# A recurrent-attention and mixture-of-experts kernel: another written-out order for its first ten steps

## The chip, the cores and the metric

The kernel runs on one core of a Trainium2 chip. The metric is the device time of one execution in microseconds (us), start to end. A core has four engines that each work through an instruction queue of their own, in order: PE (matrix products), DVE (vector work), ACT (pointwise functions, also used for copies) and POOL (general work; here also the issue of scattered writes). SP is a fifth queue that only issues transfers. An instruction starts when it is at the head of its queue and the semaphores it waits for have come.

## The reference

The first half is a gated recurrent attention over 4 batches, 8 heads, 768 tokens and 48 dimensions; the second routes each token to one of 8 experts.

```python
f = 1.0 / (1.0 + np.exp(-f_logit))
state = np.zeros((B, H, D, D))
for t in range(S):
    state = f[:, :, t, :, None] * state + np.einsum('bhd,bhe->bhde', k[:, :, t], v[:, :, t])
    y[:, :, t] = np.einsum('bhd,bhde->bhe', q[:, :, t], state)
x = y.transpose(0, 2, 1, 3).reshape(3072, 384)
logits = x @ w_gate                       # (3072, 8)
expert_idx = np.argmax(logits, axis=1)
gate_w = softmax(logits)[expert_idx]
out = gate_w * (np.maximum(x @ w1[expert_idx], 0) @ w2[expert_idx])   # per expert, 384 -> 1024 -> 384
```

## The kernel before

The tokens are cut into twelve units (u = 0 to 11), each 128 tokens of two batches with all heads. A unit has two halves, a and b, of four head pairs each. The recurrence inside a unit becomes matrix products; between units a state is carried, with two chains (units of equal parity follow each other). All steps below are written in program order under a manual schedule, so what stands first in the program stands first in each engine's queue.

The work of one unit, with the short names that the changed kernel gives it:

- SP: `lf`, `lk`, `lq`, `lv` load f, k, q, v (0.5, 0.5, 0.5 and 0.375 MB). Buffers are few (f 2, k 3, q 4, v 3), so a load waits until the unit that used the buffer has been read.
- ACT: `exp` and `ln` (log of the decay, L495 and L503), later `r` (growth, L524) and `dec` (decay, L539), both from the running sum; `keep` copies the turned k out of PSUM (L582), `set` copies y out of PSUM (L652), `lay` copies rows out (L707, L712).
- DVE: `sum` (running sum by a scan, L510), `q` (q times decay, L551), `mx` and `my` (causal masks of the two heads of a half, L568), `upd` (new state, L642 or L644), `lg` (logits, L690), and the routing chains `oh` (choose an expert, L228 to L236) and `place` (positions, L247 to L274).
- POOL: `kr` (k times growth, L528; for units 0 and 3 it runs on DVE instead, `krv`), the small copies `ends` (L534) and `last` (L546), the state's decay `upd..p` (L646), `line` (token numbers of a group), and `send`: two scattered row writes to `xs` in memory (L195).
- PE: `sc` (scores, L562), `kp` (k turned by the identity, L577), `wi` (y from inside the unit, L590), `dp` (the state's increment, L627), `bef` (y from the carried state, L611), `xp` (rows and logits from y, L682; every second unit two small counting products, L240 and L241).

Step n works on several units at once: PE does `sc(n)`, `kp(n)`, `wi(n-1)` first half, `xp(n-2)`, `wi(n-1)` second half, `dp(n)`, `bef(n-1)`. Steps 1 to 3 have extra conditions of their own in the loop (`if n == 1`, `1 < n < 4`, ...); from step 4 on all steps are alike until step 10. Two units make a group, whose tokens are routed together and sent by scatters in later steps.

PSUM sets two rings. `sc` takes four banks, two for each half, so a half's scores need the masks of the same half one unit earlier. `kp` a and b, `xp` a and b and `dp` take turns in two banks (`turns`), so each of them needs the last but one of that list to have been read: by `keep`, by `lg` and `lay`, or by `upd`. The output `yt` of `wi` and `bef` is one tile of two banks, a half in each.

Some `kr` are made to wait for a DVE instruction by hand, with the reason given as "the port of both":

```python
        def by_r(u, part=whole, on=nc.gpsimd):
            k = units[u]["k"][:, part]
            ins = on.tensor_tensor(k, k, units[u]["r"][:, part], op=OP.mult).ins
            if routed and on is nc.gpsimd:
                tc.add_manual_dep(ins, routed.pop().name, SYNC, reason="the port of both")
```

Before the first scores PE runs 24 products on zeros (`warm(24)`, L729, called `fill24` below), and 8 more after `kp(0)`.

After the twelve units come two steps without new units, with the first products of experts 0 and 1 (their rows are read back from `xs` as `xrow`, L289, which waits for the scatters sent so far), and then the eight experts in a row, all on PE (L336, L352, L1121, L1147). The first two experts' weights `w1t` and `w2t` are loaded at the end of steps 8 and 9.

Of the kernel before, what the change touches and what calls it, by code (L numbers as in the profile page):

```python
# [19 lines left out]
C = 128  # L20
# [100 lines left out]
def kernel(  # L121
# [318 lines left out]

    with ExitStack() as st:
# [7 lines left out]
        yt = psy.tile([128, 2, HP, C], F32, name="yt")  # L449
        nc.vector.memset(yt, 0.0)  # L450
# [119 lines left out]
        def keys(u):  # L570
            x = units[u]
            x["kn"] = wk.tile([128, SEG, C], F32, name="kn", bufs=1)
            x["kp"] = []
            for a in range(2):
                kp = turns("kp", [128, HP, C])
                for p in range(HP):
                    nc.tensor.transpose(kp[:, p], x["k"][:, HP * a + p], ident)  # L577
                x["kp"].append(kp)

        def keep(u):  # L580
            for a in range(2):
                nc.scalar.copy(units[u]["kn"][:, HP * a : HP * a + HP], units[u]["kp"][a])  # L582

        def within(u, a):

            x = units[u]
            if a == 0:
                x["yt"] = yt
            for p, h, _ in heads():
                nc.tensor.matmul(  # L590
                    x["yt"][DP * (h ^ a) : DP * (h ^ a) + D, a, p],
                    lhsT=x["v"][:, a, 2 * p + h],
                    rhs=x["at"][:, a, h, p],
                    start=p == 0,
                    stop=x["old"] is None,
                    skip_group_check=True,
                )

        def before(u):
# [6 lines left out]
            for p in range(HP):  # L606
                for h in range(2):
                    for a in range(2):
# [3 lines left out]
                            x["yt"][to : to + D, a, p],  # L612
# [7 lines left out]
        def added(u):  # L620
# [3 lines left out]
            for a in range(2):  # L624
                for p, h, r in heads():
# [3 lines left out]
                        lhsT=x["kn"][:, s, r],  # L629
# [6 lines left out]
        def update(u):  # L636
# [3 lines left out]
            last = _bc(x["last"], 2, D)  # L640
# [5 lines left out]
            return lambda: nc.gpsimd.tensor_tensor(new, new, last, op=OP.mult)  # L646

        def settle(u):
            x = units[u]
            x["ys"] = wk.tile([128, 2, HP, C], F32, name="ys", bufs=1)  # L650
            for a in range(2):
                nc.scalar.copy(x["ys"][:, a], x["yt"][:, a])  # L652
# [10 lines left out]
        def rows(u, counted=None):  # L663
# [11 lines left out]
            x["xr"], x["xp"] = group["xr"][:, 2 * (u - g[0]) :], []  # L675
            for a in range(2):
                j = 2 * (u - g[0]) + a
                xp, counts = pair()
                if a and counted:
                    counted.count(counts[:, :, 0 : counted.n])  # L680
                for p in range(HP):
                    done["rows"] = nc.tensor.matmul(  # L682
                        xp[:, p],
                        lhsT=x["ys"][:, a, p],
                        rhs=wx[:, p, 0:XW] if a else wx[:, p, E:WX],
                        start=True,
                        stop=True,
                    ).ins
                gate = slice(0, E) if a else slice(2 * D, XW)
                nc.vector.reduce_sum(  # L690
                    group["lg"][:, j],
                    xp[:, :, gate].rearrange("p h e -> p e h"),
                    axis=AX_X,
                )
                x["xp"].append(xp)
# [4 lines left out]
        def lay(u):  # L700

            x = units[u]
            for a in range(2):
                to = x["xr"][:, a, 0:DM].rearrange("p (h w) -> p h w", h=HP)
                if a:
                    for h in range(2):
                        nc.scalar.copy(  # L707
                            to[:, :, D * h : D * h + D],
                            x["xp"][a][:, :, XW - D * h - D : XW - D * h],
                        )  # L710
                else:
                    nc.scalar.copy(to, x["xp"][a][:, :, 0 : 2 * D])  # L712
# [4 lines left out]
        load(0, "f", ab)  # L717
        load(0, "k")
        load(1, "f", ab[:1])
        load(0, "q")  # L720
        load(1, "f", ab[1:])
        load_first_consts()
        load(1, "kq")
        for i in (1, 0):
            nc.gpsimd.memset(scores[i], 0.0)
        def warm(count):

            for _ in range(count):
                nc.tensor.matmul(yt[:, 0, 0], lhsT=pad[:, 0:C], rhs=pad[:, 0:C], start=True, stop=True)  # L729

        warm(24)
        for part in ab:
            steps(0, part)
            total(0, part)
        load(2, "f")
        load(0, "v")
        for part in ab:
            growth(0, part)
            by_r(0, part, nc.vector)
            decay(0, part)  # L740
        for part in ab:
            by_decay(0, part)
        ends(0)
        last_decay(0)
        lay_selection()
        for part in ab:
            steps(1, part)
        load(3, "f")
        load(2, "k")
        load(1, "v")  # L750
        load(2, "q")
        load_gate()
# [42 lines left out]
        score(0, 0)  # L795
        score(0, 1)
        keys(0)
        warm(8)
        for part in ab:
            total(1, part)  # L800
        for a, part in enumerate(ab):
            growth(1, part)
            by_r(1, part)
            decay(1, part)
            for h in range(2):
                mask(0, a, h)
            scaled = by_decay(1, part)
            if a == 0:
                routed.append(scaled)
        ends(1)  # L810
        last_decay(1)
        steps(2)
        load(4, "f")
        load(3, "k")
        load(3, "q")
        load(2, "v")
        total(2)
        keep(0)
        steps(3, logs=False)
        growth(2)  # L820
        load(5, "f")
        load_consts()

        for n in range(1, NU + 2):
            here, back, last = n, n - 1, n - 2
            ahead = n + 1 < NU
            state = n < NU - 2
# [3 lines left out]
            if 2 < last:  # L831
                settle(last)
# [5 lines left out]
            if ahead and not 1 < n < 4:  # L838
                by_r(n + 1)
                ends(n + 1)  # L840
# [9 lines left out]
            if n == 1:  # L850
                units[0]["old"] = None
                added(0)
                update(0)()
            if ahead and not 1 < n < 4:
                decay(n + 1)
                last_decay(n + 1)
            if state:
                keys(here)
                keep(here)
            if 1 < n < 4:  # L860
                growth(n + 1)
                if n == 3:
                    by_r(n + 1)
                ends(n + 1)
                decay(n + 1)
                last_decay(n + 1)
            if here < NU:
                for a in range(2):
                    for h in range(2):
                        if n == 2 and a and h:  # L870
                            by_r(n + 1, on=nc.vector)
                        mask(here, a, h)
            if n == 1:
                log(3)
                within(0, 0)
                within(0, 1)
                settle(0)
            if n == 1:
                steps(4, logs=False)
            elif n > 3 and n + 3 < NU:  # L880
                steps(n + 3)
# [3 lines left out]
            if 3 < n < NU - 2:  # L885
                total(n + 2)
            if n == NU - 2:
                by_decay(n + 1)
            first_half = 1 < n < NU - 2
            if first_half:  # L890
                within(back, 0)
            if 0 <= last:
                rt = rows(last, later[1] if later else None)
                lay(last)
            if 1 < n < 4:
                log(n + 2)
                steps(n + 3, logs=False)
# [5 lines left out]
            if ahead and n < NU - 2:  # L903
                by_decay(n + 1)
            if n == 2:
                total(n + 2)
            if rt and n != 3:
                rt.choose()
                if 3 < n < NU - 2:
                    routed.append(rt.latest)  # L910
                if n >= NU - 1:
                    rt.weigh()
            if later:
                settled(*later)
                routed.append(later[1].latest)
                later = None
            for a in range(int(first_half), 2):
                if 0 < back < NU:
                    within(back, a)
            if n == 2:  # L920
                settle(1)
            if n + 2 < NU and n > 3:
                growth(n + 2)
# [4 lines left out]
            if state:  # L928
                added(here)
                decayed = update(here)  # L930
            if n == 1:
                total(3)
            if n == 3:
                total(5)
                rt.choose()
                routed.append(rt.latest)
            if back < NU:
                before(back)
            if n == 3:
                settle(2)  # L940
                log(6)
                growth(5)
# [425 lines left out]
```

## Time and profile before

| | us |
|---|---|
| three runs of the kernel | 389.91, 390.06, 401.82 |
| their median | 390.06 |
| the profiled execution, its own time | 393.27 |
| its span, first to last instruction | 391.5 |
| PE busy in the span | 377.9 (97%) |
| DVE, ACT, POOL busy | 171.0, 102.8, 113.7 |
| scores of unit 0 start | 9.94 |
| scores of unit 2 start | 23.88 |
| scores of unit 10 start | 99.16 |
| first full expert product (L336, `hps`) | 144.59 |

The mean granted TensorE clock is 0.996. The attention part is the first third of the span; the rest is the experts. Times in the trace are counted from the span's start. A line of the timeline gives start, length, engine, line and operation, the tiles, and in square brackets how long the engine had stood idle before and what released it; "x16" is a run of 16 instructions shown as one. A busy PE may still be short of its peak.

### The profile page before, as it was taken

To read this page: it belongs to the slowest core of one execution; us is meant where nothing else is said; L and a number is where in the kernel's file an instruction comes from. 1 tells how busy PE (TensorE), PEld (TensorE's weight loads), DVE (VectorE), ACT (ScalarE), POOL (GpSimd) and SP (SyncE) were. 2 spreads that over 40 slices of the span, in tenths; PEclk is the share of its full clock that TensorE was granted. 3 is DMA by queue.
4 is the path that set the end of the run, shared out by engine and by line. 5 is a ranking of instruction groups with operands and counts; after the bars stand their busy time and mean duration, and the time that the engine had idled before them with its cause. 6 is when DMAs were issued, how large, how long until landed. Compare 5 with 4: busy or idle time off the path is not lost.

```text
span 391.5 us, 7712 instructions
## 1 busy us (share of the span) xinstructions
PE 377.9 (97%) x3054; PEld 264.7 (68%) x3054; DVE 171.0 (44%) x366; ACT 102.8 (26%) x190; POOL 113.7 (29%) x120
## 2 busy tenths in 40 slices
PE   7899999999999999999999999999999999999993
PEld 7887888999989678685555555654466466464452
DVE  6998998979663632112121131116413013111450
ACT  7887977775432001010100110000010010001000
POOL 5772688897645310100001001000100100100011
PEclk9999999999999999999999999999999999999998
DMA  7999657778982359694549999898173469992231
GB/s 276 384 396 359 206 200 256 233 223 315 395 295 106 127 157 321 166 322 101 191 123 397 237 399 395 201 401 236 40 260 94 101 233 387 404 407 95 80 122 42
DMA packets 51659, 94.81 MB, mean 242 GB/s; under 512 B 20840, under 2 KB 40875, under 8 KB 49568
## 3 DMA queue, kind: packets, MB, share of 16 engines
q1 hardware_dynamic: 48448, 84.62, 64.0%
q0 software_dynamic: 3168, 9.64, 6.6%
q8 instruction: 25, 0.41, 0.4%
q14 instruction: 18, 0.15, 0.1%
HBM read 79.23 MB, written 15.21 MB: 241 GB/s over the span
## 4 chain that ended last, share of the span: by engine, by line
PE 84%; DVE 8%; issue 2%; DMA 2%; ACT 1%; POOL 1%; SPq 0%; POOLq 0%; DVEq 0%; ACTq 0%
PE hps L336 28%; PE yps L352 24%; PE yps L1147 7%; PE xp L682 5%; PE yt L590 4%; PE s L562 4%; PE s L336 3%; DVE sum L510 3%; PE hps L1121 3%; PE yt L611 2%; PE yp L352 2%; DVE at L568 2%; DMA q<-in_qu_dram 2%; DVE q L551 1%; PE kp L577 1%
## 5 line engine op out<-in xcount | busy, mean ns | idle before, releaser
L336 PE MATMUL hps<-xT,w1t 128*128 128x352 f32 (+2 forms) x384 | 110.1, 447 | 0.0
L336 PEld LDWEIGHTS hps<-xT,w1t 128*128 128x128 f32 x384 | 72.7, 190 | 37.2 <-issue 1.9
L352 PE MATMUL yps<-w2t,hT 128*128 128x384 f32 x288 | 94.4, 487 | 0.0
L195 POOL DMA_INDIRECT out_dram<-ysb,dst x24 | 23.4, 975 | 224.4 <-DVE ysb L363 214.7
L352 PEld LDWEIGHTS yps<-w2t,hT 128*128 128x128 f32 x288 | 54.6, 190 | 38.6 <-issue 1.5
L346 ACT ACTIVATE hT<-hps 128x352 f32<-128x352 f32 (+2 forms) x28 | 13.8, 491 | 200.4 <-PE hps L336 171.7
L348 DVE TENSOR_SCALAR hT<-hps 128x352 f32<-128x352 f32 (+2 forms) x28 | 15.6, 558 | 93.0 <-PE hps L336 93.0
L363 DVE TENSOR_SCALAR ysb<-yps,tg 128x384 f32<-128x384 f32 x22 | 13.6, 618 | 74.4 <-PE yps L352 55.6
L195 POOL DMA_INDIRECT xs<-xr,posi x24 | 32.9, 1371 | 18.7 <-issue 4.3
L568 DVE COPY_PREDICATED at<-mpack,s 128x512 f32<-128x512 uint8 x48 | 31.3, 727 | 4.9 <-PE s L562 4.9
L510 DVE TENSOR_TENSOR_SCAN sum<-g,cap 128x1032 f32<-128x1032 f32 (+1 forms) x14 | 28.9, 2070 | 2.6 <-ACT g L503 2.6
L528 POOL TENSOR_TENSOR k<-k,r 128x1024 f32<-128x1024 f32 (+1 forms) x11 | 24.1, 2190 | 14.1 <-ACT r L524 7.1
L1147 PE MATMUL yps<-qw,hqT 128*32 128x192 f32 (+1 forms) x192 | 27.5, 381 | 0.3 <-issue 0.2
L562 PE MATMUL s<-q,k 64*128 64x128 f32 x384 | 24.9, 279 | 1.8 <-POOL rend L534 1.3
L682 PE MATMUL xp<-wx,ys 128*128 128x104 f32 x192 | 25.2, 281 | 0.9 <-ACT kn L582 0.7
L562 PEld LDWEIGHTS s<-q,k 64*128 64x128 f32 x384 | 22.5, 188 | 3.9 <-issue 1.9
L590 PE MATMUL yt<-at,v 128*48 128x128 f32 x384 | 25.1, 276 | 0.0
L682 PEld LDWEIGHTS xp<-wx,ys 128*128 128x128 f32 x192 | 22.7, 191 | 2.8 <-issue 1.4
L590 PEld LDWEIGHTS yt<-at,v 128*48 128x48 f32 x384 | 20.0, 123 | 2.6 <-issue 1.5
L1147 PE MATMUL yps<-w2t,hT 128*32 128x384 f32 x192 | 21.4, 487 | 0.0
L551 DVE TENSOR_TENSOR q<-q,g 128x1024 f32<-128x1024 f32 (+1 forms) x14 | 16.5, 1188 | 0.3 <-DMA q<-in_qu_dram 0.3
L1147 PEld LDWEIGHTS yps<-w2t,hT 128*32 128x32 f32 x192 | 7.6, 110 | 13.0 <-issue 12.5
(116 smaller groups left out, 362.5 us busy)
## 6 DMA issues: line engine op xcount, KB each, us to landing
qw<-in_moe_w_dram SPq DMA_DIRECT2D x16, 1536.0 KB
w1t<-in_moe_w_dram SPq DMA_DIRECT2D x8, 1536.0 KB
w2t<-in_moe_w_dram SPq DMA_DIRECT2D x8, 1536.0 KB
k<-in_ku_dram SPq DMA_DIRECT2D x12, 512.0 KB
q<-in_qu_dram SPq DMA_DIRECT2D x12, 512.0 KB
f<-in_fu_dram SPq DMA_DIRECT2D x10, 512.0 KB
xs<-pad SPq DMA_DIRECT2D x8, 600.0 KB
v<-in_vu_dram SPq DMA_DIRECT2D x12, 384.0 KB
```

Source lines behind the costliest of these rows:

```text
L195: ins = nc.gpsimd.indirect_dma_start(out=dst, out_offset=bass.IndirectOffsetOnAxis(ap=idx, axis=0), in_=src, in_offset=None, bounds_check= ...
L336: nc.tensor.matmul(x["h"][:, f], lhsT=w[0][:, j, b * 128 : b * 128 + 128], rhs=x["xT"][:, j], start=j == 0, stop=j == KD - 1,)
L348: nc.vector.tensor_scalar(to, x["h"], 0.0, None, op0=OP.max)
L352: nc.tensor.matmul(yp, lhsT=x["hT"][:, f, t * C : t * C + C], rhs=w[1][:, f, :], start=f == 0, stop=f == NF - 1,)
L510: nc.vector.tensor_tensor_scan(x["sum"][:, part].rearrange("p s c -> p (s c)"), x["g"][:, part].rearrange("p s c -> p (s c)"), cap[:, part ...
L528: ins = on.tensor_tensor(k, k, units[u]["r"][:, part], op=OP.mult).ins
L551: return nc.vector.tensor_tensor(q, q, x["dec"][:, part], op=OP.mult).ins
L562: done["score"] = nc.tensor.matmul(ps[h][:, p], lhsT=x["k"][r, s], rhs=x["q"][r, s], start=True, stop=True).ins
L568: nc.vector.copy_predicated(x["at"][:, a, h], _bc(causal, 1, HP), x["ps", a][h])
L590: nc.tensor.matmul(x["yt"][DP * (h ^ a) : DP * (h ^ a) + D, a, p], lhsT=x["v"][:, a, 2 * p + h], rhs=x["at"][:, a, h, p], start=p == 0, st ...
L682: done["rows"] = nc.tensor.matmul(xp[:, p], lhsT=x["ys"][:, a, p], rhs=wx[:, p, 0:XW] if a else wx[:, p, E:WX], start=True, stop=True,).ins
L1147: nc.tensor.matmul(yp[r], lhsT=h[:, f, at : at + T], rhs=w[:, f, cols], start=f == 0, stop=f == NF - 1, skip_group_check=True,)
```

## The change

Steps 0 to 9 are no longer made by the loop: a string lists every piece of work in one order, and a table maps each name to the function. The loop starts at step 10. The number and kind of the instructions stay the same.

```diff
+    FIRST = 10
+    FIRST_STEPS = """
+        lf0a exp0a ln0a lf0b exp0b ln0b sum0a dec0a sum0b r0a lk0 krv0a lf1a lq0 lf1b
+        consts0 ends0 fill24 fill8 r0b exp1a krv0b lk1 lq1 kp0a q0a dec0b q0b sc0a sc0b ln1a
+        sum1a lf2 exp1b ln1b kp0b sum1b keep0a r1a mx0a my0a lv0 lf3 dec1a dec1b krx1a r1b
+        krx1b exp2 ln2 q1a sc1a wi0a lk2 lv1 keep0b last0 exp3 dp0 kp1a mx0b my0b q1b sc1b
+        sel0 last1 set0a keep1a sum2 r2 upd0 kp1b keep1b ends1 ends2 dec2 wi0b ln3 lq2 gate0
+        dp1 kr2 mx1a lf4 lk3 exp4 ln4 my1a mx1b my1b wi1a kp2a keep2a upd1 kp2b q2 sc2a
+        last2 sum3 ends3 mx2a upd0p sc2b my2a mx2b lq3 lv2 lf5 consts1 lq4 upd1p line0 xp0a
+        lg0a set0b wi1b keep2b my2b lk4 lv3 lf6 pads0 dec3 q3 last3 r3 krv3 xp0b lay0a dp2
+        lg0b set1a set1b wi2a sc3a line1 line2 exp5 lay0b ln5 kp3a keep3a upd2 lk5 lv4 sum4
+        r4 sum5 kp3b keep3b kr4 wi2b xp1a upd2p sc3b lg1a dec4 exp6 mx3a my3a mx3b lq5 xp1b
+        lg1b lay1a lay1b bef2 r5 kr5 set2a dp3 kp4a lf7 lk6 q4 sc4a set2b upd3 kp4b ends4
+        ends5 my3b mx4a keep4a ln6 my4a wi3a oh1 dec5 sum6 wi3b bef3 keep4b q5 xp2a lg2a
+        sc4b mx4b xp2b lg2b last4 last5 ends6 exp7 ln7 my4b sc5a lv5 mx5a my5a r6 lay2a
+        upd3p dp4 sc5b set3a wi4a lq6 lf8 lk7 lv6 lq7 lf9 set3b upd4 lay2b kr6 ex1 place1
+        line3 send5 kp5a dec6 q6 exp8 sum7 keep5a kp5b keep5b wi4b xp3a lg3a lay3a xp3b
...
+        lay5b wi6b bef6 my7b sc8b oh5 ends8 r9 lv9 dec9 send7 mx8a my8a mx8b dp7 kp8a ex5
+        set6a wi7a set6b upd5p upd6p upd7 kp8b keep8a keep8b sum10 q9 lq10 line6 xp6a lg6a
+        xp6b lg6b wi7b dec10 q10 lay6a lay6b lk11 lv10 place5 last8 kr9 sc9a exp11 my8b mx9a
+        my9a bef7 set7a r10 dp8 upd8 lq11 kr10 lw0 kp9a wi8a set7b sc9b mx9b my9b ln11 wi8b
+        lww0 lv11 line7 lw1 lww1 keep9a kp9b ends9 keep9b xp7a xp7b bef8 lg7a lay7a upd7p
+        sum11 upd8p send8 send9 lg7b oh7 ends10 last9 last10 r11 dp9 lay7b upd9
+    """
...
-        yt = psy.tile([128, 2, HP, C], F32, name="yt")
-        nc.vector.memset(yt, 0.0)
+        yt = [psy.tile([128, HP, C], F32, name=f"yt{a}") for a in range(2)]
+        for y in yt:
+            nc.vector.memset(y, 0.0)
...
-            x["kn"] = wk.tile([128, SEG, C], F32, name="kn", bufs=1)
+            x["kn", a] = wk.tile([128, HP, C], F32, name=f"kn{a}", bufs=1)
...
-            x["ys"] = wk.tile([128, 2, HP, C], F32, name="ys", bufs=1)
-            for a in range(2):
-                nc.scalar.copy(x["ys"][:, a], x["yt"][:, a])
+            for a in halves:
+                x["ys", a] = wk.tile([128, HP, C], F32, name=f"ys{a}", bufs=1)
+                nc.scalar.copy(x["ys", a], x["yt"][a])
...
+        def do_by_r_behind(u, part):
+            routed.append(latest[0])
+            by_r(u, piece(part))
...
-        for n in range(1, NU + 2):
+        for what, u, part in re.findall(r"([a-z]+)(\d+)([abp]?)", FIRST_STEPS):
+            DO[what](int(u), part)
+        routed.append(routes[FIRST - 3].latest)
+        later, decayed = (FIRST - 1, routes[FIRST - 3]), waiting.pop(FIRST - 1)
+
+        for n in range(FIRST, NU + 2):
```

So `kp`, `keep`, `set`, `rows` and `lay` become separate calls for the two halves; the tiles for the copied k, the settled y and y's two banks are split by halves; `kp` often stands ahead of `sc`; both fills stand ahead of the first scores; only `krx1a`, `krx1b` and `krx8` (by `do_by_r_behind`) still wait for a DVE instruction by hand, while `kr2`, `kr4` to `kr7`, `kr9` and `kr10` do not. SP's queue holds the same transfers in the same order as before. From step 10 on the loop's body does what it did.

## Prediction

> **What bounds the kernel now.** I read the page first, then the chain of waits, then the timeline engine by engine up to 131 us.
>
> ```profile
> span 391.5 us, 7712 instructions
> PE 377.9 (97%) x3054; PEld 264.7 (68%) x3054; DVE 171.0 (44%) x366; ACT 102.8 (26%) x190; POOL 113.7 (29%) x120
> ```
>
> PE is busy nearly all the time, so an order can win only what PE loses. The chain shows what a dense step (here step 7) costs PE:
>
> ```profile
> 71.39 1.99 PE s L562 x32
> 73.38 1.02 PE kp L577 x8
> 74.40 1.01 PE yt L590 x16
> 75.41 1.96 PE xp L682 x16
> 77.38 1.01 PE yt L590 x16
> 78.39 0.92 PE dp L627 x32
> 79.31 1.33 PE yt L611 x32
> 80.64 1.99 PE s L562 x32
> ...
> 85.73 0.16 PE xp L240 x2
> 85.89 0.22 PE xp L241 x2
> ```
>
> Unit prices: `sc` 1.99, `kp` 1.02, `wi` 2 x 1.01, `xp` 1.96 (0.38 more with counts), `dp` 0.92, `bef` 1.02 (1.33 here, 1.02 in even steps). Two steps are 2 x 8.93 + 0.38 = 18.24 by these; the trace takes 18.63 (71.39 to 90.02). So a dense pair hides 0.39 of excess. The open waits stand earlier, in PE's timeline:
>
> ```profile
> 9.94 2.06 PE L562 MATMUL s<-q,k 64*128 64x128 f32 x32 [0.21 <-DVE q L551]
> ...
> 12.86 1.95 PE L729 MATMUL yt<-pad 128*128 128x128 f32 x16
> 15.04 1.16 PE L562 MATMUL s<-q,k 64*128 64x128 f32 x16 [0.24 <-issue]
> 16.95 1.16 PE L562 MATMUL s<-q,k 64*128 64x128 f32 x16 [0.74 <-POOL rend L534]
> ...
> 35.45 0.66 PE L577 MATMUL kp<-fpack,k 128*128 128x128 f32 x4 [0.55 <-DVE state L644]
> ...
> 46.72 1.14 PE L682 MATMUL xp<-wx,ys 128*128 128x104 f32 x8 [0.67 <-ACT kn L582]
> ```
>
> From 62 us to 113 none is left.
>
> **The ceiling.** What PE has to do from the first scores to `sc(10)` at 99.2: ten `sc` 19.9, ten `kp` 10.2, nine `wi` 18.2, eight `xp` 15.7, three counts 1.1, ten `dp` 9.2, seven `bef` 7.1, together 81.4; with `fill8` (1.95) 83.4. It had 89.3 (9.94 to 99.2). So 5.9 us are lost, by waits and excess. No work is removed, and from step 10 on the order is the old one, so 5.9 (1.5%) is about all that can be won.
>
> **The start.** Both fills now precede the first product. 24 fills ended at 9.72; eight more at 1.95 end at 11.67, so unit 0's scores start 1.73 later, and the 1.95 that stood at 12.86 is gone: floor for `sc(10)` 11.67 + 81.4 = 93.1, against 93.3 for the old arrangement without loss.
>
> **Walking the new order.** I went through the four queues with durations from the timeline (DVE: scan half 1.21, whole 2.25; `q` 0.62 / 1.13; a mask 0.62; `upd` 0.48; `oh` 1.1; `place` 1.65. ACT: whole `exp` 1.16, whole `ln`, `r`, `dec` 0.97, each half 0.54, `keep` and `set` 0.48 a half, `lay` 0.4. POOL: `kr` 2.33, half 1.3, `upd..p` 0.8). I note where PE stands.
>
> - ACT: `keep0a` now precedes `r1a` and needs `kp0a`, done at 12.2. Behind it wait `r1a` (12.7 to 13.3; before 11.81), `dec1a`, `dec1b`, `exp2` (14.9; before 14.10). DVE hardly notices: it scans until 12.93, its masks start at 13.25 when the scores are there (before 12.93), and `q1a` ends at 15.1 to 15.3. PE, through with `kp0b` at 14.7, waits 0.7 for it: nothing fills this hole now.
> - `dp0` needs `keep0b`, which stands behind `ln2` (17.0 to 17.5): 0.2. `kp1b` needs a bank of the ring of two, so `upd0`, which stands behind `sum2` (17.2 to 19.45) on DVE: 20.0, 0.05.
> - `kr2` ends at 23.05, and `kp2` starts after `wi1a` at 23.5; `q2` is done at 24.2, `sc2` starts at 24.5. Before, `sc2` started at 23.88, but now `wi1a` and `kp2` (2.03) are already behind it: 1.4 ahead.
> - Step 3: `dp2` needs `lay0a` (29.0), reached at 29.5; `sc3a` needs `krv3` (DVE, 31.35) and is reached at 31.4; `xp1b` needs `keep3b` (35.75), reached at 36.5; `dp3` needs `lay1a` (38.3), reached at 38.5. No wait of size, where the old order waited 0.55 and 0.25.
> - Steps 4 to 9: `kp4a` needs `kr4` (37.6, or 38.9 if it must first let `sum5` end, as `last` did at 16.80 with 2.21 under a scan), reached at 39.4; `kp5b` needs `upd4` (50.6), reached at 52.2; `kp6b` needs `upd5` (59.1), reached at 60.1; `sc7a` needs `q7` (65.4), reached at 66; `sc8b` needs `my7b` (74.9), reached at 75.9; `kp9b` needs `upd8` (87.5), reached at 89.6. Every margin is 0.1 to 2 us. DVE stays full, but `sum5` is done at 36.5 (before 43.9), which is the slack.
> - Transfers: SP's queue is the same and its buffers come free a little sooner (`v4` waits for `wi1b`, 28.5 against an issue at 30.98), but `lk7` goes out at 46.4, behind `sc4b` (before 45.10), with `lv6`, `lq7` and `lf9` behind it. They are needed by 57, so this costs nothing; a landing over 8 us would be late for `kr7`.
>
> Waits found: 0.95. So 94.1 by the walk. To it come excesses that the walk has not: 0.39 a pair of steps stays, over four pairs 1.6 (bounds 0, if the half tiles remove it, and 3.2, if it doubles); and after a wait a group runs longer (`dp` 1.07 instead of 0.92 at 50.40), 0.15 for each of about six restarts, 0.9 (bounds 0.3 and 2). `sc(10)` at 96.6 against 99.2: **2.6 us won**.
>
> **Contention of DVE and POOL** is what the walk can least see. Rows of before:
>
> ```profile
> 37.76 2.37 POOL L528 TENSOR_TENSOR k<-k,r 128x1024 f32<-128x1024 f32 x1 [1.39 <-ACT r L524]
> 39.22 1.99 DVE L551 TENSOR_TENSOR q<-q,g 128x1024 f32<-128x1024 f32 x1
> 68.59 1.22 DVE L551 TENSOR_TENSOR q<-q,g 128x1024 f32<-128x1024 f32 x1
> 75.15 3.02 POOL L195 DMA_INDIRECT xs<-xr,posi  x1 [0.16 <-issue]
> 102.14 1.04 POOL L195 DMA_INDIRECT xs<-xr,posi  x1 [0.15 <-issue]
> ```
>
> A `q` that meets a `kr` takes 0.77 longer; a scattered write that meets a scan takes 2 longer. Seven `kr` are no longer held behind a DVE instruction. By my walk they mostly fall on masks and scans, which lie beside `kr` in the old trace without stretching it (2.39 at 20.26, over four masks). Bounds: 0 and 7 x 0.77 = 5.4, of which DVE's slack before the masks takes the first 2 to 3. I take 0.
>
> A rule speaks against this part: the Trainium skill, "SBUF — State Buffer", section "Who interferes with whom", says that a DVE instruction with two SBUF inputs and a POOL instruction that reads SBUF exclude each other for the whole of the one that started first. The rows agree in kind (the `q` at 39.22 ends about 1.0 after the `kr`). As an estimate by that rule, each of the seven might hold DVE for up to a `kr`, 7 x 2.33 = 16.3; that sum would be some 14 slower than mine. Its size is not in the numbers used here.
>
> **What is given back after step 9.** On POOL `kr10` stands behind `r10`, which stands on ACT behind `set7a`, so behind `bef7`: about 89 to 91.3. Behind it wait `ends9`, `upd7p`, `upd8p` (93.1), `send8`, `send9` (4.4 and 2.8 by the rows at 93.78 and 102.14: 100.3), three copies, then the loop's `kr(11)` (103.3; before 101.06), needed by `sc(11)` at 103.9; then step 10's scatters to 107.1 (before 104.9). The read-back `xrow` waits for their landing, 5.1 us in the old trace (104.9 to 110.03, beside the weight loads, which now end some 2.6 earlier). Then five issues (2.9), the landing, and the turn, which began at 117.76 and is now wanted at 115.2. With a landing of 2 it is in time; with 5.1 it is up to 1.8 late. I take 0.3.
>
> **Sum.** 2.6 - 0.3 = 2.3 won. The profiled span of 391.5 becomes 389.2; its execution took 393.27, 3.2 above the median of the runs (390.06), a disturbance that I leave out by taking 2.3 from the median: **387.8 us**.
>
> **Rivals.**
> 1. *The new order is as dense as it can be:* the excess of 1.6 goes too (y's halves in tiles of their own), and restarts cost 0.3. `sc(10)` at 94.4, 4.8 won: 385.3. For it: the walk finds no wait after 20 us. Against: the excess also stands in steps where nothing is waited for.
> 2. *Given back:* `kr(11)` or `xrow` comes late, since POOL's queue at the end of step 9 is later than before though PE is earlier. PE then meets the same end as before: 2.6 - 2.6 = 0, 390.1. For it: margins of 0.6 and less. Against: the weight loads are out of the way sooner.
> 3. *Slower, by the ring of two banks:* every `kp` b needs an `upd` that stands in DVE's queue behind a 2.25 us scan or masks. The row at 35.45 shows the price where it is late: PE idle 0.55, its weight queue 0.79. If it is late in each of nine steps, 9 x 0.79 = 7.1 on top of 94.1 + 2.5: `sc(10)` at 103.7, 4.5 lost, 394.6. It decides once DVE lags the walk by 1 us, which two or three stretched `q` would do; lateness of 1.2 in each step would make it over 2%. Against: in the walk `upd` is ready 0.5 to 2 early from step 4 on.
>
> That the change does not do what it says is excluded for the order: it is manual, and the string gives each queue its sequence.
>
> **How the numbers follow.** Forecast (386.3 to 389) 0.5; rival 1, and anything below 386.3, 0.13; rival 2 (389 to 391.3) 0.2; rival 3 0.17. The likeliest gives 387.8. The range leaves out the best of rival 1 and the worse part of rival 3: 385 to 392.5. A measurement of this kernel tells about 2%, 7.8 us, from no change. Faster by that needs more than the 5.9 that PE loses: 0.04, for a mistake in my ceiling. Slower by it needs most of rival 3 and more: 0.09. Within: 0.87.
>
> **What would show it.** Right: PE's first scores near 11.7, one hole of 0.7 near 15, `sc2` near 24.5, no PE wait above 0.3 from 24 us on, `sc(10)` near 96.6, the experts' `hps` near 142.3, DVE busy above 90% from 10 to 60 us. Wrong: PE waiting for DVE's `state` before `kp` (rival 3), `q` of 1.9 in most steps (contention), or PE waiting for `xT` near 117 (rival 2).

## The result, and the profile after

The changed kernel takes 391.97 us (median of 17 runs), the kernel before 389.91 us on the same chip: a ratio of 1.0065 (1.005 to 1.008). It is 2.1 us slower where 2.3 us were to be won. By the bound of 2% it is no change; by the measurement's own interval it is a small loss.

The first trace of the kernel before comes from an execution 3.4 us above its median, that of the changed kernel from one at its median, so the two spans (391.5 and 390.2) point the wrong way. The reading therefore goes by start times on PE. A second trace of each, taken later on one of the chips of the experiments, has the same ones within 0.2 us.

| PE starts, us | before | predicted | after |
|---|---|---|---|
| first scores | 9.94 | 11.7 | 11.04 |
| `sc(2)` | 23.88 | 24.5 | 24.14 |
| `sc(10)` | 99.16 | 96.6 | 100.79 |
| `sc(11)` | 106.46 | 103.9 | 108.56 |

The head of the page of after: PE's busy time has risen by 1.0 though no product was added, so some of its instructions took longer. DVE has one instruction more, as y's banks are zeroed one by one.

```profile
span 390.2 us, 7692 instructions
PE 378.9 (97%) x3054; PEld 264.9 (68%) x3054; DVE 174.7 (45%) x367; ACT 102.3 (26%) x190; POOL 107.0 (27%) x120
```

PE's timeline of after (start, duration, engine, line, operation; in brackets the idle time ahead and what ended it):

```profile
11.04 2.06 PE L594 MATMUL s<-q,k 64*128 64x128 f32 x32
...
15.02 1.16 PE L594 MATMUL s<-q,k 64*128 64x128 f32 x16 [1.34 <-POOL k L560]
...
24.14 2.06 PE L594 MATMUL s<-q,k 64*128 64x128 f32 x32
...
80.12 0.66 PE L607 MATMUL kp<-fpack,k 128*128 128x128 f32 x4
82.92 1.49 PE L618 MATMUL yt<-at,v 128*48 128x128 f32 x16 [2.15 <-ACT ys L681]
...
100.79 2.06 PE L594 MATMUL s<-q,k 64*128 64x128 f32 x32
...
108.56 2.06 PE L594 MATMUL s<-q,k 64*128 64x128 f32 x32 [0.40 <-DVE lg L728]
```

The profile puts the wait at 15.02 down to POOL's `krx1a`, but that had ended at 14.07. `q1a` ended at 14.81, and `sc1a` starts 0.21 behind it, as far behind as in the kernel before (14.83 and 15.04). From 15 us to 80 us there is no wait of size, as the walk had it. Then PE stands idle for 2.15 us ahead of `wi7a`, and that is the only large hole. The chain of waits of after goes through DVE exactly there; its longest piece there is one small routing instruction:

```profile
76.23 0.65 DVE at L600
76.88 0.07 DVE mx L229
76.95 0.02 issue
76.98 4.39 DVE eq L230
...
82.05 1.93 DVE at L600 x3
83.98 0.45 DVE state L671
84.43 0.04 issue
84.48 1.12 PE kp L607 x4
```

The timelines of DVE, POOL and ACT of after around it:

```profile
76.98 4.38 DVE L230 TENSOR_TENSOR eq<-lg,mx 128x32 f32<-128x32 f32 x1
81.39 0.19 DVE L231 TENSOR_TENSOR eq<-eq,fpack 128x32 f32<-128x32 f32 x1
...
77.03 1.63 POOL L673 TENSOR_TENSOR state<-state,last 128x384 f32<-128x384 f32 x2
78.59 0.20 POOL L702 COPY xr<-fpack 128x4 f32<-128x4 f32 x1
78.72 0.15 POOL L703 MEMSET xr<- 128x56 f32 x1
78.81 0.18 POOL L578 COPY last<-g 128x8 f32<-128x8 f32 x1
78.96 2.34 POOL L560 TENSOR_TENSOR k<-k,r 128x1024 f32<-128x1024 f32 x1
...
82.17 0.23 ACT L269 ACTIVATE ex<-ex 128x32 f32<-128x32 f32 x1 [3.46 <-DVE ex L237]
82.30 1.05 ACT L681 COPY ys<-yt 128x512 f32<-128x512 f32 x2
```

`oh5` on DVE begins with `eq`, an instruction of 128x32 elements that takes 0.19 elsewhere. Here it takes 4.38, from the start of POOL's series `upd5p`, `upd6p`, `line6`, `last8`, `kr9` to its end at 81.30. On ACT `ex5` waits for `oh5`, `set6a` stands behind `ex5`, and PE's `wi7a` needs `set6a`. On DVE three masks and `upd7` stand behind it, and PE's `kp8b` needs `upd7`.

The hole costs more than itself. Stretches of after (window, its length, then busy time of each engine, granted PE clock, DMA share, GB/s):

```profile
core 0: us, PE busy (x) PEld busy (x) DVE busy (x) ACT busy (x) POOL busy (x), PEclk, DMA share, GB/s
80.70:82.90 2.20, 0.08 (x1) 0.00 (x0) 2.10 (x7) 0.73 (x3) 0.60 (x1) 1.00 0.20 78
83.50:86.80 3.30, 3.23 (x21) 2.80 (x18) 3.30 (x4) 1.07 (x3) 0.00 (x0) 0.50 0.06 11
87.00:100.00 13.00, 13.00 (x224) 11.41 (x222) 9.76 (x24) 7.31 (x13) 6.22 (x6) 1.00 0.76 274
```

From 83.45 to 86.86, for 3.41 us after the hole, PE's granted clock is 0.50; `wi7a`, 1.08 elsewhere, takes 1.49. At half speed 3.41 us lose 1.7.

A second meeting stands at the end. Rows of POOL of before, then of POOL and DVE of after:

```profile
90.32 2.37 POOL L528 TENSOR_TENSOR k<-k,r 128x1024 f32<-128x1024 f32 x1 [1.62 <-DVE some L780]
...
98.71 2.35 POOL L528 TENSOR_TENSOR k<-k,r 128x1024 f32<-128x1024 f32 x1 [0.30 <-PE dp L627]
```

```profile
93.32 2.37 POOL L560 TENSOR_TENSOR k<-k,r 128x1024 f32<-128x1024 f32 x1 [12.02 <-ACT r L556]
...
104.06 2.35 POOL L560 TENSOR_TENSOR k<-k,r 128x1024 f32<-128x1024 f32 x1
...
106.51 0.82 POOL L673 TENSOR_TENSOR state<-state,last 128x384 f32<-128x384 f32 x1
...
104.66 3.76 DVE L583 TENSOR_TENSOR q<-q,g 128x1024 f32<-128x1024 f32 x1
```

`kr10` had to wait for `r10`. Between it and `kr(11)` POOL now has two scatters (`send8` and `send9`, four writes) where the old order has one, so the two stand 10.74 apart after and 8.39 before. POOL is late, and `q11` (1.2 alone) ran into `kr(11)` and `upd9p`. From `sc(10)` to `sc(11)` it is 7.77 now, 7.30 before: 0.47 lost.

### The profile page after: what moved, and what is told of

Same layout as the page of the kernel before. It is cut to its first block, busy times and chain, and to the rows that moved or that the text cites. A ratio compares the mean times of both kernels' runs of the same rounds, so it can differ in the third digit from the quotient of the medians.

```text
span 390.2 us, 7692 instructions
## 1 busy us (share of the span) xinstructions
PE 378.9 (97%) x3054; PEld 264.9 (68%) x3054; DVE 174.7 (45%) x367; ACT 102.3 (26%) x190; POOL 107.0 (27%) x120
## 4 chain that ended last, share of the span: by engine, by line
PE 90%; DVE 5%; DMA 2%; ACT 1%; issue 1%; POOL 1%; SPq 1%; POOLq 0%
PE hps L337 28%; PE yps L353 24%; PE yps L1143 7%; PE xp L717 5%; PE s L594 5%; PE yt L618 5%; PE s L337 3%; PE hps L1117 3%; PE yp L353 3%; PE kp L607 3%; PE dp L655 2%; PE yt L639 2%; DMA f<-in_fu_dram 2%; DVE at L600 1%; DVE eq L230 1%; DVE q L583 1%
## 5 line engine op out<-in xcount | busy, mean ns | idle before, releaser
L196 POOL DMA_INDIRECT xs<-xr,posi x24 | 30.0, 1249 | 16.5 <-issue 4.9
L560 POOL TENSOR_TENSOR k<-k,r 128x1024 f32<-128x1024 f32 (+1 forms) x11 | 25.3, 2300 | 21.6 <-ACT r L556 21.6
L542 DVE TENSOR_TENSOR_SCAN sum<-g,cap 128x1032 f32<-128x1032 f32 (+1 forms) x14 | 27.8, 1997 | 1.7 <-ACT g L535 1.6
L594 PE MATMUL s<-q,k 64*128 64x128 f32 x384 | 26.5, 282 | 1.7 <-POOL k L560 1.3
L717 PE MATMUL xp<-wx,ys 128*128 128x104 f32 x192 | 26.4, 286 | 0.2 <-ACT ys L681 0.2
L717 PEld LDWEIGHTS xp<-wx,ys 128*128 128x128 f32 x192 | 23.8, 197 | 1.8 <-issue 0.9
L583 DVE TENSOR_TENSOR q<-q,g 128x1024 f32<-128x1024 f32 (+1 forms) x14 | 17.4, 1245 | 0.6 <-DMA q<-in_qu_dram 0.6
```

Of the source, the lines that this page charges most:

```text
L196: ins = nc.gpsimd.indirect_dma_start(out=dst, out_offset=bass.IndirectOffsetOnAxis(ap=idx, axis=0), in_=src, in_offset=None, bounds_check= ...
L542: nc.vector.tensor_tensor_scan(x["sum"][:, part].rearrange("p s c -> p (s c)"), x["g"][:, part].rearrange("p s c -> p (s c)"), cap[:, part ...
L583: return nc.vector.tensor_tensor(q, q, x["dec"][:, part], op=OP.mult).ins
L594: done["score"] = nc.tensor.matmul(ps[h][:, p], lhsT=x["k"][r, s], rhs=x["q"][r, s], start=True, stop=True).ins
L717: nc.tensor.matmul(x["xp", a][:, p], lhsT=x["ys", a][:, p], rhs=wx[:, p, 0:XW] if a else wx[:, p, E:WX], start=True, stop=True,)
```

## The experiments

Theory: the order is as good as predicted, and one meeting of DVE's `eq` with POOL's series took away more than it won (2.15 of waiting, 1.7 of halved clock). Rivals: the tiles by halves cost something themselves; the removal of the hand-set holds costs at many places, not one; the ring of two banks (`kp` waiting for `upd`) is the bound. The runs below were taken on three chips, on which the kernel before takes 392.2 to 393.2 us. Each is compared by its ratio to the kernel before on the same chip. The expected times of "oh5 later", "kr9 held", the old order written out and the kernel before without its holds were reckoned from the first chip's 389.91 and are to be read as ratios to that.

### oh5 later

```diff
-  sc8b oh5 ends8
+  sc8b ends8
...
-  kp8a ex5 set6a wi7a set6b upd5p upd6p upd7 kp8b keep8a keep8b
+  kp8a set6a wi7a set6b upd5p upd6p upd7 oh5 kp8b keep8a keep8b ex5
```

> The new order with oh5 moved behind upd7 on DVE and ex5 behind keep8b on ACT; nothing else changes. Theory A (in the new order the comparison eq of oh5, 4.38 us instead of 0.19 at 76.98, stood shut out by POOL's unbroken series upd5p, upd6p, line6, last8, kr9 until 81.30, and all that PE lost against the old order after step 8 follows from it): the eq takes under 0.6 us, PE's idle time of 2.15 us before wi7a is gone, sc(10) starts at 96.8 to 97.5 instead of 100.79, and the time is 388 to 389, about 3 below the new order. Theory B (the new order is too tight somewhere else, in the ring of two banks or in ACT's order, and the long eq only fell into slack): PE idles elsewhere in steps 7 to 9, sc(10) stays above 100 and the time at 391.5 to 392.5.

Measured: 391.24 us, ratio 0.9964 (0.9951 to 0.9978). Rows of its POOL, DVE and PE timelines:

```profile
78.87 2.36 POOL L559 TENSOR_TENSOR k<-k,r 128x1024 f32<-128x1024 f32 x1
...
76.04 1.96 DVE L599 COPY_PREDICATED at<-mpack,s 128x512 f32<-128x512 uint8 x3
...
80.20 0.56 DVE L670 TENSOR_TENSOR state<-dp,state 128x384 f32<-128x384 f32 x1 [0.40 <-PE dp L654]
...
80.89 0.39 DVE L230 TENSOR_TENSOR eq<-lg,mx 128x32 f32<-128x32 f32 x1
...
81.62 0.65 PE L606 MATMUL kp<-fpack,k 128*128 128x128 f32 x4
...
96.90 2.06 PE L593 MATMUL s<-q,k 64*128 64x128 f32 x32
...
104.67 2.06 PE L593 MATMUL s<-q,k 64*128 64x128 f32 x32 [0.40 <-DVE lg L727]
```

With two tokens moved the hole is gone and `sc(10)` starts at 96.90, 3.9 sooner than in the changed kernel. That is the 2.15 and the 1.7. Theory A holds: its 388 to 389 is 0.995 to 0.998 of 389.91. The masks, two of which now lie beside POOL's same series, keep their 0.65 each, and `upd7`, which like `eq` is a TENSOR_TENSOR, takes its usual 0.56 beside `kr9`. Both have an input in PSUM (`s`, `dp`), while `eq` has both in SBUF.

### kr9 held

```diff
-  upd5p upd6p upd7 kp8b ... lq10 line6 xp6a ... place5 last8 kr9 sc9a
+  upd5p upd6p line6 last8 krx9 upd7 kp8b ... lq10 xp6a ... place5 sc9a
```

`krx9` is `kr9` held by hand behind `oh5`, as it is in the kernel before; everything else stays.

> The new order with one hold more: line6, last8 and kr9 are placed right behind upd6p in the list, and kr9 waits by hand for oh5. DVE's order stays as it is. Theory A: POOL's series before the hold is only upd5p, upd6p and two copies, 2.0 us, so the eq of oh5 takes 1.9 to 2.2 us instead of 4.38, ends near 79, and kr9 runs from about 80 to 82.4 beside the masks; the wait of PE before wi7a falls from 2.15 to under 0.4; time 388 to 389.5. Theory A' (the eq is late because of the scattered writes of send7, which end at 77.0, and not because of the TENSOR_TENSORs): the eq still takes over 4 us and the time stays at 391.5 to 392.5.

Measured: 391.87 us, ratio 0.9976 (0.9957 to 0.9995), `sc(10)` at 96.83. DVE's and POOL's rows:

```profile
76.69 1.75 DVE L230 TENSOR_TENSOR eq<-lg,mx 128x32 f32<-128x32 f32 x1
...
76.75 1.64 POOL L672 TENSOR_TENSOR state<-state,last 128x384 f32<-128x384 f32 x2
...
79.45 2.37 POOL L559 TENSOR_TENSOR k<-k,r 128x1024 f32<-128x1024 f32 x1 [0.73 <-DVE ex L237]
```

`eq` still waits out the two state updates (1.64), but not the rest of the series, and DVE and ACT have slack for that. So POOL's series is the cause, from its own side, and the long `kr9` is the part of it that matters. Theory A' falls: the scattered writes of `send7` stand where they stood.

### ex5 alone later

The hole has two chains, one through ACT (`ex5`, `set6a`, `wi7a`), one through DVE (masks, `upd7`, `kp8b`). Here only ACT's is cut:

```diff
-  kp8a ex5 set6a wi7a set6b upd5p upd6p upd7 kp8b keep8a keep8b
+  kp8a set6a wi7a set6b upd5p upd6p upd7 kp8b keep8a keep8b ex5
```

> The changed kernel with one token moved: ex5 (ACT, 0.23 us) stands behind keep8b instead of ahead of set6a. oh5 stays on DVE where it meets POOL's series. This parts the loss into two chains. Theory A (the hole of 2.15 us at wi7a comes through ACT alone, since ex5 waits for oh5 and set6a stands behind ex5; DVE's own lateness costs about 1 us, because kp8b waits for upd7): eq is again some 4.4 us, wi7a starts without a wait near 80.8, PE waits about 1.0 us for upd7 ahead of kp8b, no half clock, sc(10) near 98.2 and sc(11) near 106.0, 0.998 to 1.000 of the kernel before. Theory B (DVE's lateness sets everything, ACT is only the messenger): sc(10) at 100.5 or later as in the changed kernel, 1.005.

Measured: 395.86 us, ratio 1.0102 (1.0081 to 1.0122): slower than the changed kernel itself. Rows of DVE and PE, and a stretch (PEclk is third from the end):

```profile
77.14 4.40 DVE L230 TENSOR_TENSOR eq<-lg,mx 128x32 f32<-128x32 f32 x1
...
82.23 1.92 DVE L599 COPY_PREDICATED at<-mpack,s 128x512 f32<-128x512 uint8 x3
84.05 0.55 DVE L670 TENSOR_TENSOR state<-dp,state 128x384 f32<-128x384 f32 x1
...
84.65 0.66 PE L606 MATMUL kp<-fpack,k 128*128 128x128 f32 x4 [2.69 <-DVE state L670]
...
85.40:92.00 6.60, 6.60 (x41) 6.04 (x42) 5.02 (x12) 3.78 (x8) 0.00 (x0) 0.50 0.22 82
```

Theory A of this run fell: it forgot the three masks between `oh5` and `upd7`. `wi7a` starts on time, then `kp8b` waits 2.69 for `upd7`. DVE sets the time; ACT was only the nearer messenger. And the hole, longer by 0.54, is now followed by 6.8 us at half clock in place of 3.41, another 1.7: `sc(10)` at 103.02. This is the clearest row on the clock's part: 2.15 idle plus 1.7 gave 3.9, 2.69 plus 3.4 gives 6.1, and `sc(10)` is 6.1 behind that of "oh5 later" (0.3 of it stands already at `sc8b`, ahead of the hole: 78.13 and 77.86).

### The old order, written out

A list that gives each of the five queues the sequence of before; only the tiles by halves are left of the change.

```diff
-  lf0a exp0a ln0a lf0b exp0b ln0b sum0a dec0a ...
+  lf0a lf0b lk0 lf1a lq0 lf1b consts0 lk1 lq1 fill24 exp0a ln0a ...
```

> The new code with a list that gives every queue exactly the old order (holds by hand included): only the split of the copied k, the settled y and y's banks into half tiles is left of the change. Theory A: the split costs and brings nothing, time 389.4 to 390.4, ratio to the old kernel 0.998 to 1.002. Theory C (the split itself costs, through more semaphores, and the order brings its predicted 2.3): 391 to 394. Theory D (the split brings something, as finer waits let PE run): 387.5 to 389.

Measured: 393.81 us, ratio 1.0047 (1.0027 to 1.0068). Theory A falls; the time is that of theory C. Its trace has `sc(11)` at 106.28, so up to there nothing is lost. The loss lies later. From `sc(11)` to `hps` it takes 38.86 (before 37.97), and two waits of PE there are 1.78 together (in before, two waits ahead of `yp`, 0.52 and 0.33):

```profile
126.97 0.37 PE L241 MATMUL rp<-oh,fpack 128*128 128x16 f32 x2 [0.97 <-DVE mx L229]
...
129.13 5.43 PE L353 MATMUL yp<-w2t,hT 128*128 128x384 f32 x16 [0.81 <-ACT hT L347]
```

That is half of the loss of 1.8; where the other half arises is not shown.

### The old order, with the copied k alone in halves

```diff
-  yt = [psy.tile([128, HP, C], F32, name=f"yt{a}") for a in range(2)]
+  yt = psy.tile([128, 2, HP, C], F32, name="yt")
...
-  x["ys", a] = wk.tile([128, HP, C], F32, name=f"ys{a}", bufs=1)
-  nc.scalar.copy(x["ys", a], x["yt"][a])
+  if a == 0:
+      x["ys"] = wk.tile([128, 2, HP, C], F32, name="ys", bufs=1)
+  nc.scalar.copy(x["ys"][:, a], x["yt"][:, a])
```

> The old order of every queue, with the copied k alone in tiles by halves; y's bank and the settled y are each one tile. The old order with all three split took 1.0047 of the kernel before, though its sc(11) stood at 106.28 against 106.5. Theory A (the loss comes through y and ys, which are in use until 125 us, while kn's last use is in step 9): 1.000 to 1.001. Theory B (it comes through kn, or through the code's being written out): 1.004 to 1.005.

Measured: 392.5 us, ratio 1.0003 (0.9992 to 1.0015). Theory A holds. So writing the order out and splitting `kn` cost nothing, and the halves of `yt` and `ys` cost about 0.4% in the old order (the two runs are of two chips, each against the kernel before on its own). Why they cost it behind 123 us is not settled.

### The new order with all tiles joint, and with oh5 later too

The same edit as in the last run, and `kn` in one tile as well; in the second run with the moves of "oh5 later".

```diff
-  x["kn", a] = wk.tile([128, HP, C], F32, name=f"kn{a}", bufs=1)
+  if a == 0:
+      x["kn"] = wk.tile([128, SEG, C], F32, name="kn", bufs=1)
```

> The new order with y's bank, the copied k and the settled y each in one tile again: the split into tiles by halves is taken back, the order stays. The old order with split tiles took 1.0047 of the kernel before. Theory A (the split costs about 0.47% whatever the order): 1.0065 - 0.0047 = 1.002 of the kernel before, 393.4. Theory B (the split pays with this order, because with one tile the halves wait for each other): PE waits at kp, wi or xp in steps 2 to 9 and more than 1.0065. Theory C (the split is neutral, the loss of the old order with split tiles was of another kind): 1.006 to 1.007.

> The new order with oh5 behind upd7 (and ex5 behind keep8b) and with the tiles joint again. With split tiles this order took 0.9964. Theory A (the split costs 0.47% whatever the order): 0.9964 - 0.0047 = 0.9917, 389.4, about the 3 us that the prediction expected of the order. Theory B (the split pays with this order): above 0.9964. Theory C (neutral): 0.995 to 0.998.

Measured: 397.06 us, ratio 1.0117 (1.0102 to 1.0132), and 396.33 us, ratio 1.0094 (1.0074 to 1.0115). Theory B holds: the order needs the halves, and without them it loses 0.6% and 1.3% more. PE waits 1.96 and 1.97 ahead of `kp5`; the next run but one shows why.

### Both meetings addressed

`oh5` and `ex5` as above; besides, `r10` moves up on ACT, with `last8 kr9` ahead of it in the list because `r` has one buffer, and `kr10` is held behind `place5`.

```diff
-  dec10 q10 lay6a lay6b lk11 lv10 place5 last8 kr9 sc9a exp11 ... set7a r10 dp8 upd8 lq11 kr10
+  dec10 last8 kr9 r10 q10 lay6a lay6b lk11 lv10 place5 krx10 sc9a exp11 ... set7a dp8 upd8 lq11
```

> The changed kernel with both meetings of DVE and POOL taken out: oh5 behind upd7 and ex5 behind keep8b (as before, alone 0.9964), and r10 on ACT behind dec10 instead of behind set7a, with kr10 held behind place5. POOL then starts kr10 about 1 us sooner (88.4 against 89.44), is through with step 9's scatters sooner, and kr(11), which is held behind oh7, ends before q11 starts. Theory A (PE's start of sc(11) sets the time): q11 of 1.2 to 2 us instead of 2.9, sc(11) at 104.3 instead of 104.67, 0.995 to 0.996 of the kernel before. Theory B (behind sc(11) the gain is lost again, PE's signals near 124 us): sc(11) as in A, but 0.997 or more.

Measured: 390.16 us, ratio 0.9947 (0.9929 to 0.9965), the fastest of all. The added part did not do what it was for:

```profile
89.57 2.37 POOL L559 TENSOR_TENSOR k<-k,r 128x1024 f32<-128x1024 f32 x1 [7.82 <-DVE some L783]
...
102.08 2.98 DVE L582 TENSOR_TENSOR q<-q,g 128x1024 f32<-128x1024 f32 x1
...
105.20 2.06 PE L593 MATMUL s<-q,k 64*128 64x128 f32 x32 [0.40 <-DVE lg L727]
```

`kr10` now waits for the hold instead of for `r10` and starts no sooner (89.57; 89.44 in "oh5 later"). `q11` meets `kr(11)` as before, and from `sc(10)` to `sc(11)` it is 7.76 again; POOL comes to `kr(11)` 11.1 behind `kr10`, past `send8` and `send9`. From `sc(2)` to `sc(11)` it takes 80.63, and 80.64 in "oh5 later", and its interval overlaps that run's. So the added moves won nothing that is shown, and the gain is `oh5`'s.

### The same order, y joint, kn in halves

> The order of the last experiment (oh5 and ex5 later, r10 sooner; 0.9947) with y's bank and the settled y each in one tile again, the copied k still in halves. In the old order the split of y and ys cost 0.4% (1.0047 against 1.0003). Theory A (it costs that in any order): 0.9907, sc(10) near 97.0. Theory B (the new order needs these halves, because it settles one half while the other is still in use): PE waits for ys or yt at wi or xp in steps 2 to 9, sc(10) at 98 or later and 0.997 or more. With all tiles joint the order lost 5 us at sc(11); what is left of this with kn split tells which of the splits the order needs.

The edit is that of "the copied k alone in halves". Measured: 394.61 us, ratio 1.0043 (1.0025 to 1.006), `sc(10)` at 102.11. ACT's and PE's rows:

```profile
54.05 0.59 ACT L680 COPY ys<-yt 128x512 f32<-128x512 f32 x1 [3.69 <-PE yt L616]
...
55.97 1.06 PE L605 MATMUL kp<-fpack,k 128*128 128x128 f32 x8 [1.96 <-DVE place L260]
```

Theory B again. The new order issues `wi4a` ahead of `set3b`. With one tile, `set3b` has to let `wi4a`'s products into the other half of the bank end (54.05, against 49.05 with halves); behind it stand the rows that `place1` waits for, and `kp5` needs the bank that `place1` reads. Waits of 0.35, 0.37 and 0.59 follow in later steps. So it is y's halves that this order needs.

### The kernel before without its holds

```diff
-  if routed and on is nc.gpsimd:
+  if False:
```

In `by_r`, so no `kr` is held behind `choose` or `place` any more; the order is the old one.

> The old kernel with all its holds by hand taken out: no kr waits for a DVE instruction any more. Theory A (a DVE instruction with two inputs in SBUF, such as q, the eq of oh or the scan, waits for as long as POOL has such work back to back): in steps 4 to 10 some of q, oh and place stretch by 1 to 3 us each where kr now starts earlier; DVE has 1.1 us of slack in a step, so the time rises by 1 to 5, to 391 to 395. Theory E (the holds cover only a rare case, and kr mostly falls beside masks, as the prediction took it): within 0.5 of the old kernel, 389.4 to 390.4.

Measured: 397.23 us, ratio 1.0116 (1.0097 to 1.0134). Theory A holds. Three of the routing's `oh` (0.19 alone) now meet a `kr`, for example:

```profile
63.43 2.36 DVE L232 TENSOR_TENSOR oh<-fpack,val 128x32 f32<-128x32 f32 x1
```

The holds are worth 1.2% in the old order. There they let the small routing instructions go first; the change dropped five of them and paid at one, that of `kr9`.

### Both kernels once more

> The kernel before, unchanged, for a second trace of it on the chip on which the others are timed. Its first trace lies 3.4 us above its median. Theory A (the whole of that is a stall near 124 to 131 us that only some executions have): first scores near 9.9, sc(11) near 106.4 and hps near 144.4 as in the first trace if the stall is there, about 142.5 if it is not. Theory B (the difference lies behind hps, in the experts' part): hps near 144.4 again, and the span differs behind it.

> The changed kernel, unchanged, on the chip of the experiments, so that they can be compared with it directly. If the ratio to the kernel before is a property of the two kernels, it is again near 1.0065, that is 395.2 against 392.7. If the two chips differ in it, it may be 1.000 to 1.010. Trace: oh5's eq of 4.4 us near 77 beside POOL's series and PE idle 2 us at wi7a should be there again, since the order of every queue is fixed; the half clock after it is expected only if the gap is again about 2 us.

Measured: the kernel before 392.35 us, with `sc(11)` at 106.53 and `hps` at 144.44, as in its first trace, and a span shorter by 1.0 (theory B); the changed kernel 393.86 us, ratio 1.0056 (1.003 to 1.0082), with `eq` and the hole of 2.15 again, the half clock after it, `sc(11)` at 108.72 and `hps` at 146.62. From `sc(11)` to `hps` both take 37.9 here. In the first trace of the changed kernel it was 36.6, so the lateness of 2.2 at `sc(11)` is the loss, and it goes through to the end.

All together, with the lateness of `sc(11)` against 106.5 set beside the measured ratio (0.01 is 3.9 us):

| run | `sc(10)` | `sc(11)` | late, us | ratio |
|---|---|---|---|---|
| changed kernel, again | 100.95 | 108.72 | 2.2 | 1.0056 |
| oh5 later | 96.90 | 104.67 | -1.8 | 0.9964 |
| kr9 held | 96.83 | 104.60 | -1.9 | 0.9976 |
| ex5 alone later | 103.02 | 110.79 | 4.3 | 1.0102 |
| both meetings addressed | 97.44 | 105.20 | -1.3 | 0.9947 |
| old order, all halves | 98.98 | 106.28 | -0.2 | 1.0047 |
| old order, kn in halves | 99.06 | 106.36 | -0.1 | 1.0003 |
| new order, joint | 103.88 | 111.65 | 5.1 | 1.0117 |
| new order, joint, oh5 later | 101.65 | 109.42 | 2.9 | 1.0094 |
| fastest, y joint | 102.11 | 109.41 | 2.9 | 1.0043 |
| before without holds | 103.66 | 110.96 | 4.5 | 1.0116 |

The time follows `sc(11)` within 1.2 us, but for the old order with all halves, which is 2 us slower than its `sc(11)` says.

## Why the prediction was wrong, by its own steps

- **What can be won, and the walk: right within 1 us.** With the meeting taken out, `sc(10)` starts at 96.90 and 96.83; predicted were 96.6. From the end of the hole near 15 to `sc(10)` it takes 82.0 and 82.1; by the prediction it was 81.2 (from 14.7 and 0.7 of waiting to 96.6). Up to 80 us no wait above 0.3 stands behind the one near 15.
- **The start: off by 1.1 us, without effect.** The fills end near 10.5, not 11.67. The first one starts at 1.57 (at 1.57 in every trace with y's banks in halves, at 2.10 or 2.11 in every other, before too), and the granted clock is full from 4.95 on (6.35 before). The 11.7 for the first scores also leaves out `kp0a`, which the list puts ahead of them; they start at 11.04. The hole near 15 takes all this up: it is 1.34 for 0.7, since it ends with `q1a`, done at 14.81 (predicted 15.1 to 15.3).
- **Contention: this step failed.** "I take 0" was 3.9 us at `sc(10)`, of which 2.15 is waiting and 1.7 halved clock. The bound was made from a `kr` that meets a `q` (0.77 each). It also counted seven `kr` that lose their hold. They are five (`kr5` to `kr7`, `kr9`, `kr10`): in the kernel before, nothing is in `routed` when `kr2` and `kr4` are made, so these two had no hold to lose (nor had `kr1a`, which has one now). In the same terms the bound is 3.9, not 5.4, and the estimate by the skill's rule 11.7, not 16.3. The place that cost the time was of another kind: a small routing instruction, which looks harmless at 0.19, against a series of six POOL instructions, with ACT's `ex5` and DVE's `upd7` queued behind it. No row of the working looked at `eq` beside `kr9`. The reading that `kr` lies beside masks and scans without stretching holds for masks alone: beside a scan a `kr` of half length took 1.49 before (12.58; its twin 1.28), and `kr4` took 3.21 after, though PE did not wait for it. The walk checked margins against durations, but a margin of 0.1 to 2 us does not cover a lateness of 4.2.
- **The rule that spoke against it.** The row, 0.19 stretched to 4.38, agrees in kind with the Trainium skill, "SBUF — State Buffer", section "Who interferes with whom": two SBUF inputs on DVE and a reading POOL instruction exclude each other. The rows add that this series, issued back to back, kept DVE out for all of it, and that masks from PSUM run beside it. The estimate of 16.3 by that rule was too high: up to 110 us, of DVE's `q` and its routing instructions only `eq` (beside one of the `kr` that lost their hold) and `q11` (beside `kr(11)`, which kept its hold) were stretched.
- **The halved clock: not in the sum at all.** The kernel before does not show it: from 6.35 to 388.64 its granted clock is full, and its longest hole is 0.74.
- **What is given back after step 9: right in size, wrong in place.** 0.47 against 0.3. `kr10` waited for `r10`, and with `send8` and `send9` behind it POOL was late for `kr(11)`, as foreseen; the loss came through `q11`, not through the read-back. `xT` was in time.
- **The rivals.** Rival 3's rows did show, PE waiting for `upd` ahead of `kp` (2.69 in "ex5 alone later", hidden behind the wait for `ys` in the changed kernel), but at one step, not in each; its mechanism, a DVE queue that lags, was right, its cause was one stretched instruction. The half tiles, whose cost I took as nothing but an excess of PE, turned out to be needed by the order and to cost 0.4% in the old one.

## What to carry to other kernels

When a written-out order drops holds between DVE and POOL, go through each small two-input DVE instruction as well as the large ones, and ask what runs on POOL at that moment, for how long without a gap, and which engines stand in queue behind. A hole of 2 us on PE is to be priced with what the clock takes after it. And where halves of a step are interleaved, tiles must be split the same way, or the order waits for halves that it doesn't use.

## What the runs showed of the hardware that was not expected

- **The clock after a hole.** In every trace the granted clock changes only on a grid of 3.413 us, counted from where it first becomes full (half clock from 83.45 to 86.86 in after, 23 such intervals behind 4.95). In the holes seen, what counts is how much of one interval of this grid PE stands idle: 1.62 us ("kr9 held", a hole of 2.05 across a border), 1.92, 2.04 and 2.15 were each followed by one interval at half clock, 2.69 by two; 1.51 ("new order, joint, oh5 later") and 1.48 (a hole of 1.96 across a border in "new order, joint") by none. The Trainium skill, "TensorE: Matmul & The Clock Gate", section "What's actually happening", has a free-running window of 3413 ns, which agrees, and the clock dropping after at least one idle window, which does not: here less than half a window of idleness was enough, and the measurement decides.
- **PE's signals near 124 to 134 us.** In every trace but the first of the changed kernel, DVE's `counts` starts 1.1 to 2.4 us after the product of PE that it needs seems to have ended. In "oh5 later" and "kr9 held" this left PE idle for 2.04 and 2.05 ahead of `yp` and halved the clock there, so that `hps` started at 145.32 and 145.14 although `sc(11)` was 1.8 ahead of the kernel before. These two executions took 1.7 and 1.6 more than their kernels' medians. The traces with the lateness lack some records of semaphores (DVE's 300 of 317 in the kernel before), the one without it lacks none of DVE's. What causes it, and whether the profiling has a part in it, is open.
